# Attention and mixture-of-experts chain: V summed on VectorE, GpSimd and VectorE steps of the attention stage spread out, eight weight conversions moved

## The chip, the core and the metric

The kernel runs on one core of one Trainium2 chip. The metric is the device time of one launch in microseconds (us). The kernel before took 918.85 us, the median of three runs (917.21 to 921.72).

In what follows PE is TensorE, DVE is VectorE, ACT is ScalarE, POOL is GpSimd, and SP is SyncE, which here does nothing but issue DMAs. PEld is PE's weight load, which overlaps its matmuls.

## The reference, cut to what matters

Three stages, each fed by the one before it. Attention keeps only the keys whose six hash bits equal the query's; the first expert layer is a dense layer with a hard swish; the second layer picks two of eight experts per token.

```python
q_bucket = sum(((q @ proj) > 0) * 2**bits)          # 2 x 8 heads, 768 rows, 64 wide
scores = where(q_bucket == k_bucket, scale * q @ k.T, -1e9)
attn = exp(scores - scores.max(-1)); attn /= attn.sum(-1) + 1e-9
x = (attn @ v).reshape(1536, 512)
h = x @ w_in                                        # 512 -> 2048; these weights come as float64
x = (h * clip(h + 3, 0, 6) / 6) @ w_out             # 2048 -> 512
noisy = x @ w_gate + log1p(exp(x @ w_noise)) * noise
top2, w2 = two largest of noisy, softmax over them
out[n] = sum over the two experts e: w2 * (relu(x[n] @ w1[e]) @ w2[e])   # 8 experts, 512 -> 1024 -> 512
```

## The kernel before, in words

The order of instructions on PE, ACT, POOL and DVE is the order in which the Python code calls them (a manual schedule); each engine works through its own list in order, so an instruction that waits holds up all that stands behind it on its engine. SP's DMAs are put in order by the framework, and SP too issues them one after the other.

**Attention.** The 16 heads are taken in 8 pairs (NP = 8). A pair p takes 12 steps j = 0 to 11, so there are G = 96 steps g = 12p + j. The queries come in two halves of 384 (QH = 2), and each half takes six steps, one per block of 128 keys. In one step the main loop does this:

- `scores` (L469): PE multiplies keys and queries of the *next* step (L476, L477), and ACT takes the exponential of each half (L478). The S banks are two (NS = 2), so PE can be no more than one exponential ahead in each.
- `maxes` (L429): PE makes scores for a half that comes two halves later (L439), and DVE takes their row maximum (`tensor_reduce`, L443). The `mx` banks are two, so PE cannot start the maxima of step j+2 before DVE has reduced those of step j.
- in every odd step `av` (L481): PE multiplies the exponentials of two steps with V (L490). At the end of a half `finish` (L499) lets DVE add the uniform part, take the reciprocal r, and POOL write the normalised rows into `x_all` (L510).
- when a half's maxima are complete, `stab` (L445) makes the stabilisers on POOL in four short steps (L453 to L456); `stab2` (L458) has PE transpose them and ACT send them by DMA into two rows of A (L467, "A<-mr"), where the scores matmul L477 reads them.

Once per pair there are further steps, by their j: `load_cast` (0, POOL's DMA of B), `load_v` (2, the DMA of V and a POOL memset of V's ones columns), `bits_all` (4, hash bits), `lows` (6 and 7, a POOL subtraction of 128x768 each), `v_sum` (6, POOL: V summed over its six key blocks by five additions; the sum feeds the matmul of `v_sum2`), `uniform` (POOL, L342).

**Conversions.** The first layer's weights come as float64. `conv` (L186) turns half a 128-row slab into float32: it loads 512 KB (L189, "c_raw"), some steps later two ACT instructions (L200, L201) and one of DVE (L202), then one of DVE (L205) and POOL's addition (L206, 128x512), then DVE's L208, which reads what POOL wrote, and a store to DRAM (L211). There are 32. The kernel before does NU = 24 in the attention stage, one begun every three steps (g % 3 == 1), each advanced by one `yield` per step in `conv_step` (L216), and the other 8 in the first expert layer. In the attention stage a conversion's raw data take their buffer from the same pool of three as the float32 weight slabs of the first layer (tag "wr"); the first three slabs are loaded in steps 84, 85 and 86, and each gives its buffer back when `w_hi` (ACT, L229) and `w_lo` (DVE, L235) have split it, slab 0 in steps 88 and 89, slab 1 in 90 and 91, slab 2 after the last step.

**First expert layer.** 48 units u: three chunks of 512 tokens by 16 slabs, in two rounds: slabs 0 to FSPLIT-1 for each chunk, then the rest for each chunk. In a unit PE does `gemm1` for unit u+1 and `gemm2` for unit u, while ACT and DVE split slab u+2 and SP loads slab u+3. From u = 8 on a zero fill of DRAM buffers runs on SP's queue beside it (`prefill`). When a chunk is complete its routing follows in pieces (`routing`, L846).

**Second expert layer.** 10 parts by 8 slabs; the change touches only where the third chunk's routing is cut (ROUTE).

Of the kernel before, what the change touches and what calls it, by code (L numbers as in the profile page):

```python
# [20 lines left out]
EARLY = (224, 224)  # L21
ROW = 516
PF = (8, 2)
NU = 24
NS = 2
CL = 3
SL = CAP // 4
ROUTE = [(4, 0, 0), (1, 1, 0), (0, 1, 0), (4, 0, 0)]
NQ = len(EARLY)
PARTS = ([(e, 0, n, 2, False) for e, n in enumerate(EARLY)] + [(e, 0, CAP, 4, True) for e in range(NQ, 8)]  # L30
         + [(e, n, CAP - n, 2, False) for e, n in enumerate(EARLY)])
FSPLIT = 6
XA = 5
QJ = (1, 5)
XG = (75, 78, 81, 84)
# [9 lines left out]
def chain_kernel(ctx, tc, kq, vP, proj, wm, we, wgn, noise, out, dbg=None):  # L45
# [140 lines left out]
    def conv(n, cv_p, fine):  # L186
        k, hf = divmod(n, 2)
        raw = (wraw_p if fine else cv_p).tile([128, 512, 2], I32, name="c_raw", tag="wr" if fine else "c_raw")
        nc.sync.dma_start(raw, wm[k].bitcast(I32)[:, hf * 1024:(hf + 1) * 1024].rearrange("p (n t) -> p n t", t=2))  # L189
        for _ in range(CL if fine else 1):  # L190
            yield
        H, L = raw[:, :, 1], raw[:, :, 0]
        if fine:
            lu = wsp_p.tile([128, 1024], F32, name="c_lu", tag="wh")
            ta = wsp_p.tile([128, 1024], F32, name="c_ta", tag="wl")
            r, u, t, a = lu[:, :512].bitcast(I32), lu[:, 512:], ta[:, :512].bitcast(I32), ta[:, 512:]
        else:
            u, a = (cv_p.tile([128, 512], F32, name=n) for n in ("c_u", "c_a"))
            r, t = (cv_p.tile([128, 512], I32, name=n) for n in ("c_r", "c_t"))
        nc.scalar.activation(r, L.bitcast(U32), ACTF.Copy, scale=2.0 ** -29)  # L200
        nc.scalar.activation(u, H.bitcast(F32), ACTF.Abs)  # L201
        nc.vector.tensor_scalar(t, H, 3, 0x3FFFFFF8, op0=ALU.logical_shift_left, op1=ALU.bitwise_and)  # L202
        if fine:
            yield
        nc.vector.scalar_tensor_tensor(t, H, -0x40000000, t, op0=ALU.bitwise_and, op1=ALU.bitwise_or)  # L205
        nc.gpsimd.tensor_tensor(t, t, r, op=ALU.add)  # L206
        yield
        nc.vector.scalar_tensor_tensor(a, u, 2.0 ** -15, t.bitcast(F32), op0=ALU.is_ge, op1=ALU.mult)  # L208
        for _ in range(2 if fine else 1):
            yield  # L210
        nc.sync.dma_start(w32[k][:, hf * 512:(hf + 1) * 512], a)  # L211
# [68 lines left out]
    with actx:  # L280
# [35 lines left out]
        def load_v(p):  # L316
            t = T[p]
            t["V"] = op_p.tile([128, KT, 2, VW], F32, name="V", bufs=2)
            nc.sync.dma_start(t["V"], vP[p].rearrange("r k (h c) -> r k h c", h=2))
            nc.gpsimd.memset(t["V"][:, :, :, 64:], 1.0)  # L320

        def v_sum(p):
            t = T[p]
            V = t["V"].rearrange("p k h c -> p k (h c)")
            vr = sm_p.tile([128, 2 * VW], F32, name="vr")
            nc.gpsimd.tensor_tensor(vr, V[:, 0], V[:, 1], op=ALU.add)
            for k in range(2, KT):
                nc.gpsimd.tensor_tensor(vr, vr, V[:, k], op=ALU.add)
            t["vr"] = vr

        def v_sum2(p):
# [149 lines left out]
        def av(g):  # L481
            p, qh, kt = g // (2 * KT), g // KT % 2, g % KT
            t = T[p]
            if kt == 0:
                t["av"] = ps.tile([128, 512], F32, name="o", tag="o", bufs=1)
            for h in range(2):
                for i in range(KT // 2):
                    c = (h * (KT // 2) + i) * VW
                    for r in (0, 64):
                        nc.tensor.matmul(t["av"][r:r + 64, c:c + VW],  # L490
                                         E[g % NE][:, h, i * 128 + r:i * 128 + r + 64], t["V"][:, kt, h],
                                         start=kt == 0 and h == 0 and i == 0, stop=kt == KT - 1,
                                         tile_position=(0, r), skip_group_check=True)
            if kt == 0:
                at(g + 1, uniform, 2 * p + qh)
            elif kt == KT - 1:
                finish(p, qh, t["av"])

        def finish(p, qh, o):  # L499
            t = T[p]  # L500
# [6 lines left out]
            b, pp = divmod(p, NPB)  # L507
            i = b * KT + qh * (KT // 2)
            x = x_all[:, i:i + KT // 2, pp * 128:(pp + 1) * 128].rearrange("p a (h c) -> p h a c", h=2)
            nc.gpsimd.tensor_tensor(x, ov[:, :, :, 0:64],  # L510
                                    r.unsqueeze(3).to_broadcast([128, 2, KT // 2, 64]), op=ALU.mult)

        done = [0]

# [93 lines left out]
        for g in range(G):  # L608
# [51 lines left out]
                    move_k(p + 1)  # L660
            if p >= 1 and p + 1 < NP and j == 2:
                load_v(p + 1)
            if p + 1 < NP and j == 6:
                v_sum(p + 1)
                at(g + 5, v_sum2, p + 1)
            if p + 3 < NP and j == 6:
                load_raw(p + 3)
            if dbg is None or "x" not in dbg:
                conv_step(1 if g % 3 == 1 and cvn[0] < NU else 0, None, True)
            if g == 14:  # L670
                moe_consts()
            elif g == 16:
# [172 lines left out]

    def routing(c):  # L846
        for d in range(4):
            yield rt_trans(c, d)
        yield rt_logits(c)
        yield rt_noisy(c)  # L850
        yield rt_top(c)
# [2 lines left out]
        yield rt_pos(c)  # L854
        for t in range(4):
            rt_scatter(c, t)
            yield

    def w_next(k):
        if k + 3 < NMU + NEU:  # L860
# [136 lines left out]
    for u in range(NMU):  # L997
# [14 lines left out]
            w_lo(u + 2)  # L1012
        first(u + 1, lambda: w_lo(u + 2) if u else None)
        w_next(u)
        conv_step(1 - u % 2, cvm_p, False)
        route(1)
        if u + 1 < NMU:
            m1_second(u)
# [162 lines left out]
```

## Time and profile before

| | |
|---|---|
| median of 3 runs | 918.85 us |
| the profiled execution | 919.49 us, its span 917.8 us |
| PE busy | 848.0 us (92%) |
| DVE, ACT, POOL busy | 513.6, 423.1, 244.9 us |
| DMA moved | 151.74 MB, mean 165 GB/s |
| mean granted TensorE clock | 0.956 of full speed |

The table is one execution: the busy time of an engine, and the span from its first to its last instruction. The execution's time holds 1.69 us more than its span. A mean over the span hides that the stages differ: the attention stage is about the first 285 us, the first expert layer lies from there to about 560 us, and the rest is the second expert layer. The rows below cut the attention stage at the end of each pair's last V matmul.

### The profile page before, as it was taken

What the parts mean: (1) busy time and instruction counts of PE and PEld (TensorE: products, weight loads), DVE (VectorE), ACT (ScalarE), POOL (GpSimd) and SP (SyncE); (2) the same over time, 40 slices, a digit from 0 to 9 for tenths busy, and PEclk for the clock granted to TensorE, in tenths of its full rate; (3) what the DMA queues carried; (4) which work ended last, traced back from release to release, by engine and by line L of the source; (5) the groups of instructions that cost most, each with busy time, mean ns of one, the idle gap of its engine ahead of it and who ended that gap; (6) DMA issues with size and microseconds to landing.
All of it is one profiled execution on the core that took longest, in us unless ns stands there. A gap on an engine that the chain in (4) does not pass through costs nothing. (4 is left out here: it accounts for less than half of the span.)

```text
span 917.8 us, 15981 instructions
## 1 busy us (share of the span) xinstructions
PE 848.0 (92%) x6313; PEld 734.3 (80%) x6313; DVE 513.6 (56%) x859; ACT 423.1 (46%) x712; POOL 244.9 (27%) x286
## 2 busy tenths in 40 slices
PE   5889977787899999999999999889999999999993
PEld 2677766676788888888888888769999999999982
DVE  8657856565634666544665566645545445545561
ACT  4356544354555566544444444434433443443551
POOL 9166555274432121100012031521020120202211
PEclk8889998798999999999999999999999999999997
DMA  7655864945603459872225245696465666546671
GB/s 246 164 152 182 262 185 135 260 132 173 190 27 116 160 190 311 281 242 93 92 84 192 70 162 177 209 239 164 140 151 158 144 151 157 136 140 140 177 207 20
DMA packets 52347, 151.74 MB, mean 165 GB/s; under 512 B 8741, under 2 KB 9661, under 8 KB 52265
## 3 DMA queue, kind: packets, MB, share of 16 engines
q1 hardware_dynamic: 44393, 131.02, 46.6%
q0 software_dynamic: 7648, 19.53, 9.4%
q8 instruction: 51, 0.84, 0.4%
q14 instruction: 31, 0.25, 0.1%
q10 hardware_dynamic: 224, 0.10, 0.0%
HBM read 105.89 MB, written 32.41 MB: 151 GB/s over the span
## 5 line engine op out<-in xcount | busy, mean ns | idle before, releaser
L235 DVE TENSOR_TENSOR wl<-wr,wh 128x1024 fp32r<-128x1024 f32 (+1 forms) x128 | 155.9, 1218 | 126.2 <-ACT wh L229 126.2
L229 ACT CAST wh<-wr 128x1024 fp32r<-128x1024 f32 x128 | 134.4, 1050 | 120.0 <-PE S L946 75.8
L478 ACT ACTIVATE E<-S 128x384 f32<-128x384 f32 x192 | 90.5, 490 | 107.6 <-PE S L477 102.4
L976 POOL DMA_INDIRECT out_dram<-ot,ti x28 | 43.8, 1563 | 233.8 <-ACT ot L975 185.4
L443 DVE TENSOR_REDUCE mc<-mx 128x1 f32<-128x768 f32 x96 | 90.6, 951 | 19.7 <-PE mx L439 19.5
L439 PE MATMUL mx<-B,A 128*128 128x384 f32 x192 | 70.9, 383 | 27.3 <-DVE mc L443 24.9
L490 PEld LDWEIGHTS o<-V,E 128*64 128x64 f32 x2304 | 80.0, 151 | 13.8 <-issue 12.2
L273 DVE SCALAR_TENSOR_TENSOR g<-t,mx 128x512 f32<-128x512 f32 x47 | 32.4, 689 | 102.9 <-ACT t L272 102.9
L490 PE MATMUL o<-V,E 128*64 128x66 f32 x2304 | 86.8, 238 | 0.0
L701 PE MATMUL S<-wh,gh 128*128 128x512 f32 (+1 forms) x208 | 82.5, 397 | 0.0
L703 PE MATMUL S<-wh,gl 128*128 128x512 f32 (+1 forms) x208 | 81.6, 392 | 0.0
L702 PE MATMUL S<-wl,gh 128*128 128x512 f32 (+1 forms) x208 | 81.5, 392 | 0.0
L476 PE MATMUL S<-QX,KS 128*128 128x384 f32 x192 | 77.6, 404 | 2.5 <-ACT E L478 2.4
L477 PE MATMUL S<-A,B 128*128 128x384 f32 x192 | 68.8, 358 | 7.3 <-DMA A<-mr 7.3
L944 PE MATMUL S<-hh,wh 128*128 128x416 f32 x192 | 70.6, 368 | 0.0
L945 PE MATMUL S<-hh,wl 128*128 128x416 f32 x192 | 67.5, 352 | 0.0
L946 PE MATMUL S<-hl,wh 128*128 128x416 f32 x192 | 67.4, 351 | 0.0
L439 PEld LDWEIGHTS mx<-B,A 128*128 128x128 f32 x192 | 39.1, 208 | 34.6 <-DVE mc L443 30.6
L925 ACT ACTIVATE hh<-mx 128x416 fp32r<-128x416 f32 (+2 forms) x72 | 33.0, 459 | 65.6 <-PE mx L257 65.6
L272 ACT ACTIVATE t<-mx,half 128x512 f32<-128x512 f32 x47 | 32.3, 688 | 66.2 <-PE mx L257 66.2
L257 PE MATMUL mx<-xh,wh 128*128 128x512 f32 (+1 forms) x252 | 62.2, 369 | 0.6 <-ACT wh L229 0.6
L257 PE MATMUL mx<-xh,wl 128*128 128x512 f32 (+1 forms) x252 | 60.5, 362 | 0.6 <-DVE wl L235 0.6
(246 smaller groups left out, 1640.4 us busy)
## 6 DMA issues: line engine op xcount, KB each, us to landing
wr<-in_we_dram SPq DMA_DIRECT2D x80, 512.0 KB
wr<-w SPq DMA_DIRECT2D x48, 512.0 KB
c_raw<-in_wm_dram SPq DMA_DIRECT2D x32, 512.0 KB
xg<-pt SPq DMA_DIRECT2D x8, 838.5 KB
raw<-in_kq_dram SPq DMA_DIRECT2D x8, 768.0 KB
w<-c_ta SPq DMA_DIRECT2D x24, 256.0 KB
B<-in_kq_dram POOLq DMA_DIRECT2D x7, 768.0 KB, 8.2
xr<-xg SPq DMA_DIRECT2D x5, 838.5 KB
```

Of the source, the lines that this page charges most:

```text
L229: nc.scalar.copy(hi, W[k][0])
L235: nc.vector.tensor_tensor(lo[:, :n], W[k][0][:, :n], W[k][1][:, :n].bitcast(F32), op=ALU.subtract)
L257: nc.tensor.matmul(h, a[:, d * 128:(d + 1) * 128], b[:, d], start=i == 0 and d == 0, stop=i == 2 and d == 3)
L439: nc.tensor.matmul(pm[:, hf, :QW], t["A"][:, qh, q0:q0 + 128], t["B"][:, h, hf * QW:(hf + 1) * QW], start=True, stop=True)
L443: nc.vector.tensor_reduce(t["mc"][:, c:c + 1], pm[:, :, :QW], axis=AX.XY, op=ALU.max)
L476: nc.tensor.matmul(s[:, :QW], t["KS"][:, h, ks], t["QX"][:, qh, qs], start=True, stop=False)
L478: nc.scalar.activation(E[g % NE][:, h], s[:, :QW], ACTF.Exp, scale=0.125)
L490: nc.tensor.matmul(t["av"][r:r + 64, c:c + VW], E[g % NE][:, h, i * 128 + r:i * 128 + r + 64], t["V"][:, kt, h], start=kt == 0 and h == 0 ...
L701: nc.tensor.matmul(o, gh[:, ts], wh, start=first, stop=False)
L702: nc.tensor.matmul(o, gh[:, ts], wl, start=False, stop=False)
L703: nc.tensor.matmul(o, gl[:, ts], wh, start=False, stop=last)
L944: nc.tensor.matmul(o, wh[:, ds], hh, start=ft == 0, stop=False)
```

## The change

- The eight float64 conversions numbered 16 to 23 leave the attention stage (NU 24 to 16); the 16 that stay are begun every six steps (g % 6 == 3), and the first layer does 16 instead of 8. So that no slab is read before it is converted, the first round of slabs becomes longer (FSPLIT 6 to 7).
- Inside a conversion DVE's last step comes three steps after POOL's addition, not one.
- V's memset moves out of `load_v` into `v_sum`, `v_sum` moves from step 6 to step 8, and the five POOL additions become one DVE `tensor_reduce` over a strided view. `v_sum2` stays in step 11.
- POOL's write of the normalised rows is put off by one step: `finish` returns it, and it is called in the next step.
- Routing's third and fourth transposes go together, its last scatter ends the generator, and ROUTE's first entry is 3 instead of 4.

```diff
-NU = 24
+NU = 16
-ROUTE = [(4, 0, 0), (1, 1, 0), (0, 1, 0), (4, 0, 0)]
+ROUTE = [(3, 0, 0), (1, 1, 0), (0, 1, 0), (4, 0, 0)]
-FSPLIT = 6
+FSPLIT = 7
...
         nc.gpsimd.tensor_tensor(t, t, r, op=ALU.add)
-        yield
+        for _ in range(3 if fine else 1):
+            yield
         nc.vector.scalar_tensor_tensor(a, u, 2.0 ** -15, t.bitcast(F32), op0=ALU.is_ge, op1=ALU.mult)
...
             nc.sync.dma_start(t["V"], vP[p].rearrange("r k (h c) -> r k h c", h=2))
+
+        def v_sum(p):
+            t = T[p]
             nc.gpsimd.memset(t["V"][:, :, :, 64:], 1.0)
-
-        def v_sum(p):
-            t = T[p]
-            V = t["V"].rearrange("p k h c -> p k (h c)")
             vr = sm_p.tile([128, 2 * VW], F32, name="vr")
-            nc.gpsimd.tensor_tensor(vr, V[:, 0], V[:, 1], op=ALU.add)
-            for k in range(2, KT):
-                nc.gpsimd.tensor_tensor(vr, vr, V[:, k], op=ALU.add)
+            nc.vector.tensor_reduce(vr, t["V"].rearrange("p k h c -> p (h c) k"), axis=AX.X, op=ALU.add)
             t["vr"] = vr
...
             elif kt == KT - 1:
-                finish(p, qh, t["av"])
+                at(g + 1, finish(p, qh, t["av"]))
...
-            nc.gpsimd.tensor_tensor(x, ov[:, :, :, 0:64],
-                                    r.unsqueeze(3).to_broadcast([128, 2, KT // 2, 64]), op=ALU.mult)
+            return lambda: nc.gpsimd.tensor_tensor(
+                x, ov[:, :, :, 0:64], r.unsqueeze(3).to_broadcast([128, 2, KT // 2, 64]), op=ALU.mult)
...
-            if p + 1 < NP and j == 6:
+            if p + 1 < NP and j == 8:
                 v_sum(p + 1)
-                at(g + 5, v_sum2, p + 1)
+                at(g + 3, v_sum2, p + 1)
...
-                conv_step(1 if g % 3 == 1 and cvn[0] < NU else 0, None, True)
+                conv_step(1 if g % 6 == 3 and cvn[0] < NU else 0, None, True)
...
         for d in range(4):
-            yield rt_trans(c, d)
+            rt_trans(c, d)
+            if d != 2:
+                yield
...
             rt_scatter(c, t)
-            yield
+            if t < 3:
+                yield
...
-        conv_step(1 - u % 2, cvm_p, False)
+        conv_step(1 if u % 4 < 3 else 0, cvm_p, False)
```

What that does to the lists of three engines is shown by the order in which their instructions stand, an instruction to a row, with output and inputs by the program's names.

On POOL in the middle of a pair (the second one), from the end of step 5 to step 8, before; `x_all` is the write of the normalised rows, `c_ta` the conversion's addition, `ng`, `nr` and `u` the stabilisers, `KS` the two subtractions of `lows`, `vr` the sum of V:

```order
L510 TENSOR_TENSOR x_all<-ov,r 128x2x3x64
L206 TENSOR_TENSOR c_ta<-c_ta,c_lu 128x512
L453 TENSOR_SCALAR ng<-mc 128x6
L454 CAST nr<-ng 128x6
L455 TENSOR_TENSOR nr<-ng,nr 128x6
L456 TENSOR_SCALAR u<-mc 128x6
L360 TENSOR_TENSOR KS<-raw,B 128x768
L326 TENSOR_TENSOR vr<-V 128x132
L328 TENSOR_TENSOR vr<-vr,V 128x132 x4
L360 TENSOR_TENSOR KS<-raw,B 128x768
L342 TENSOR_TENSOR uf<-u,vs 128x396
L206 TENSOR_TENSOR c_ta<-c_ta,c_lu 128x512
```

and now, where `V` is the memset of its ones columns:

```order
L451 TENSOR_SCALAR ng<-mc 128x6
L452 CAST nr<-ng 128x6
L453 TENSOR_TENSOR nr<-ng,nr 128x6
L454 TENSOR_SCALAR u<-mc 128x6
L358 TENSOR_TENSOR KS<-raw,B 128x768
L508 TENSOR_TENSOR x_all<-ov,r 128x2x3x64
L358 TENSOR_TENSOR KS<-raw,B 128x768
L206 TENSOR_TENSOR c_ta<-c_ta,c_lu 128x512
L340 TENSOR_TENSOR uf<-u,vs 128x396
L324 MEMSET V 128x12x2
```

The five additions are gone, the stabilisers stand ahead of the write of `x_all`, one of two additions of a conversion is left, and the memset stands last.

On DVE over the same steps (the second pair, from the first half's end), before; `mc` is the row maximum, `ov` and `r` are the end of a half, the three rows of `c_ta` belong to conversions:

```order
L502 TENSOR_TENSOR ov<-o,uf 128x396
L505 TENSOR_SCALAR r<-ov 128x6
L506 RECIPROCAL r<-r 128x6
L205 SCALAR_TENSOR_TENSOR c_ta<-c_raw,c_ta 128x512
L443 TENSOR_REDUCE mc<-mx 128x1
L208 SCALAR_TENSOR_TENSOR c_ta<-c_lu,c_ta 128x512
L443 TENSOR_REDUCE mc<-mx 128x1
L202 TENSOR_SCALAR c_ta<-c_raw 128x512
L443 TENSOR_REDUCE mc<-mx 128x1
L205 SCALAR_TENSOR_TENSOR c_ta<-c_raw,c_ta 128x512
L443 TENSOR_REDUCE mc<-mx 128x1
L208 SCALAR_TENSOR_TENSOR c_ta<-c_lu,c_ta 128x512
```

and now, with the sum of V on it:

```order
L500 TENSOR_TENSOR ov<-o,uf 128x396
L503 TENSOR_SCALAR r<-ov 128x6
L504 RECIPROCAL r<-r 128x6
L441 TENSOR_REDUCE mc<-mx 128x1
L202 TENSOR_SCALAR c_ta<-c_raw 128x512
L441 TENSOR_REDUCE mc<-mx 128x1
L205 SCALAR_TENSOR_TENSOR c_ta<-c_raw,c_ta 128x512
L441 TENSOR_REDUCE mc<-mx 128x1
L326 TENSOR_REDUCE vr<-V 128x132
L441 TENSOR_REDUCE mc<-mx 128x1 x2
L209 SCALAR_TENSOR_TENSOR c_ta<-c_lu,c_ta 128x512
```

Before, one row maximum stands between a conversion's second and third DVE step; now three and the sum of V do.

On ACT near the end of the attention stage (steps 86 to 92 or so), before; `E` are the exponentials, `wh` the splits of the first weight slabs:

```order
L478 ACTIVATE E_132<-S 128x384 x2
L478 ACTIVATE E_133<-S 128x384 x2
L229 CAST wh<-wr 128x1024
L478 ACTIVATE E_134<-S 128x384 x2
L478 ACTIVATE E_135<-S 128x384 x2
L229 CAST wh<-wr 128x1024
L478 ACTIVATE E_132<-S 128x384 x2
```

and now:

```order
L476 ACTIVATE E_132<-S 128x384 x2
L476 ACTIVATE E_133<-S 128x384 x2
L230 CAST wh<-wr 128x1024
L476 ACTIVATE E_134<-S 128x384 x2
L476 ACTIVATE E_135<-S 128x384 x2
L200 ACTIVATE c_lu<-c_raw 128x512
L201 ACTIVATE c_lu<-c_raw 128x512
L230 CAST wh<-wr 128x1024
L476 ACTIVATE E_132<-S 128x384 x2
```

Two instructions of the conversion begun in step 87 now stand between the exponentials of step 91 and those of step 92. A further conversion (step 93) ends after the last step.

## Rows read from the trace of the kernel before

**Rows 1.** Stretches: length, busy PE, PEld, DVE, ACT, POOL; clock, DMA share, GB/s.

```profile
61.99:88.26 26.27, 25.77 (x381) 21.28 (x380) 21.01 (x32) 17.19 (x37) 16.84 (x30) 1.00 0.78 234
88.26:230.17 141.91, 115.94 (x1521) 95.30 (x1521) 88.18 (x128) 67.35 (x145) 73.30 (x101) 0.88 0.63 186
230.17:260.63 30.46, 27.72 (x378) 23.82 (x377) 19.43 (x29) 15.21 (x35) 13.64 (x23) 0.94 0.56 161
260.63:284.57 23.94, 23.02 (x353) 18.77 (x352) 6.27 (x10) 12.49 (x28) 5.98 (x8) 1.00 0.14 46
284.57:550.00 265.43, 265.43 (x1256) 218.73 (x1256) 150.40 (x264) 132.43 (x186) 33.63 (x30) 1.00 0.50 168
340.00:400.00 60.00, 60.00 (x268) 49.63 (x267) 34.57 (x47) 33.76 (x46) 5.15 (x4) 1.00 0.88 297
```

**Rows 2.** Waits from 20 to 285 us: us in total, times, longest us.

```profile
DVE c_ta L208 <- POOL c_ta L206: 59.5, 24, 6.6
...
POOL V L320 <- DMA V<-in_vP_dram: 25.2, 5, 7.6
PE mx L439 <- DVE mc L443: 23.5, 12, 3.3
```

**Rows 3.** Timeline at 157 us: start, us, instruction, idle before it.

```profile
158.49 0.69 DVE L208 SCALAR_TENSOR_TENSOR c_ta<-c_lu,c_ta 128x512 f32<-128x512 f32 x1 [4.41 <-POOL c_ta L206]
...
160.11 0.44 PE L439 MATMUL mx<-B,A 128*128 128x384 f32 x1 [2.44 <-DVE mc L443]
```

**Rows 4.** Groups of instructions, 40 to 280 us: count, busy us, mean ns.

```profile
L443 DVE TENSOR_REDUCE mc<-mx 128x1 f32<-128x768 f32 x81 | 76.9, 950 | 12.8 <-PE mx L439 12.7
...
L206 POOL TENSOR_TENSOR c_ta<-c_ta,c_lu 128x512 int32<-128x512 int32 x24 | 30.5, 1271 | 1.8 <-DVE c_ta L205 1.7
...
L360 POOL TENSOR_TENSOR KS<-raw,B 128x768 fp32r<-128x768 f32 x12 | 22.0, 1832 | 0.0
L510 POOL TENSOR_TENSOR x_all<-ov,r 128x384 f32<-128x384 f32 x15 | 17.5, 1164 | 88.2 <-DVE r L506 66.6 <-PE mx L439 14.8 <-PE S L477 6.7
...
L342 POOL TENSOR_TENSOR uf<-u,vs 128x396 f32<-128x396 f32 x15 | 13.8, 918 | 0.1
```

**Rows 5.** Timeline of POOL in pair 1: stabilisers, first subtraction, V's last additions.

```profile
81.14 0.23 POOL L453 TENSOR_SCALAR ng<-mc 128x6 f32<-128x6 f32 x1
...
82.40 1.83 POOL L360 TENSOR_TENSOR KS<-raw,B 128x768 fp32r<-128x768 f32 x1
...
84.92 2.47 POOL L328 TENSOR_TENSOR vr<-vr,V 128x132 f32<-128x132 f32 x4
```

**Rows 6.** Timeline: the stabilisers' DMA and the matmul that waits, pairs 1 and 3.

```profile
69.76 0.65 ACTq L467 DMA_DIRECT2D A<-mr  x1
...
74.93 0.44 PE L477 MATMUL S<-A,B 128*128 128x384 f32 x1 [0.50 <-DMA A<-mr]
...
130.60 0.64 ACTq L467 DMA_DIRECT2D A<-mr  x1
...
137.90 0.69 PE L477 MATMUL S<-A,B 128*128 128x384 f32 x1 [2.45 <-DMA A<-mr]
```

**Rows 7.** Timeline: a conversion's load, its first ACT step, and pair 7's steps.

```profile
162.49 1.56 SPq L189 DMA_DIRECT2D c_raw<-in_wm_dram  x1
...
165.67 0.66 ACT L200 ACTIVATE c_lu<-c_raw 128x512 int32<-128x512 uint32 x1 [2.58 <-DMA c_raw<-in_wm_dram]
...
274.60 1.23 DVE L235 TENSOR_TENSOR wl<-wr,wh 128x1024 fp32r<-128x1024 f32 x1
...
277.89 0.88 ACT L478 ACTIVATE E<-S 128x384 f32<-128x384 f32 x2 [1.16 <-PE S L477]
```

**Rows 8.** Timeline of the start: first row maxima, V's memset; PE in pair 0.

```profile
10.91 5.46 DVE L443 TENSOR_REDUCE mc<-mx 128x1 f32<-128x768 f32 x6 [0.90 <-PE mx L439]
...
11.39 0.13 POOL L320 MEMSET V<- 128x24 f32 x1
...
50.40 0.38 PE L464 MATMUL z<-ident,nr 128*12 128x128 f32 x1 [3.46 <-POOL nr L455]
```

More of the change, by code (lines that the diff above doesn't have):

```diff
@@ L319, in load_v @@
             nc.sync.dma_start(t["V"], vP[p].rearrange("r k (h c) -> r k h c", h=2))
-            nc.gpsimd.memset(t["V"][:, :, :, 64:], 1.0)
         def v_sum(p):
             t = T[p]
-            V = t["V"].rearrange("p k h c -> p k (h c)")
+            nc.gpsimd.memset(t["V"][:, :, :, 64:], 1.0)
             vr = sm_p.tile([128, 2 * VW], F32, name="vr")
-            nc.gpsimd.tensor_tensor(vr, V[:, 0], V[:, 1], op=ALU.add)
-            for k in range(2, KT):
-                nc.gpsimd.tensor_tensor(vr, vr, V[:, k], op=ALU.add)
+            nc.vector.tensor_reduce(vr, t["V"].rearrange("p k h c -> p (h c) k"), axis=AX.X, op=ALU.add)
             t["vr"] = vr
```

## The prediction

> **What bounds the kernel now.** I read the busy time by stretch first, then the waits, then the timeline at the waits.
>
> The stretches show where time can be won [rows 1]. From 284.57 to 550 us PE is busy all the time at the full clock: nothing that DVE, ACT or POOL save there can count. The attention stage is different. Pair 1 takes 26.27 us with PE busy for 25.77 at granted clock 1.00. Pairs 2 to 5 do the same work in 141.91 / 4 = 35.48 us, with PE idle for 26 of the 141.91 us and the clock at 0.88. The reader is to see that the matmuls are the same and that 9.2 us a pair are waits, and slow matmuls after them.
>
> The waits name the cause [rows 2]: PE waits 23.5 us for row maxima on DVE; DVE waits 59.5 us, 24 times, for POOL's addition of a conversion; POOL waits 25.2 us in five goes for V's DMA, because the memset of V stands in its list at step 2. So it is a chain of lists in order: POOL late, so DVE stuck at L208, so the maxima behind it late, so the `mx` banks not free. The timeline shows one link: DVE idle for 4.41 us, and PE for 2.44 soon after [rows 3].
>
> **The change part by part.** All differences are taken against the profiled execution, 919.49 us, which is 0.64 above the median of 918.85.
>
> *Pairs 2 to 5.* L208 now comes three steps after the addition instead of one. A step is about 2.1 us (26.27 / 12), so POOL may be 6 us late at no cost, and the 4.41 us wait goes. The memset leaves step 2, so POOL no longer stands behind V's DMA there. Half the conversions go: 2 additions a pair, 2 x 1.27 us off POOL [rows 4], and their DVE steps and 512 KB loads. What is left is a pair without these waits, and pair 1 is the measured example of one, with all four conversions still in it. So I start from 26.27 us, which contains a 0.50 us wait for the stabilisers' DMA [rows 6].
>
> What is late next is the sum of V. It is on DVE in step 8, waits for the memset on POOL, and the row maxima of steps 9 to 11 are queued behind it. From the start of step 6 POOL has to do: stabilisers 1.26 us (81.14 to 82.40 [rows 5]), two subtractions of 1.83, the write of `x_all` 1.16, the addition 1.27 and the uniform part 0.92 [rows 4]. That is 8.3 us. DVE comes to the sum after step 8's maxima, some 6 us after step 6 began, so it waits about 2 us. PE needs the bank of step 9 again in step 11, some 4.7 steps of 2.1 us after step 6 began, at about 9.9 us; it is free at 8.3 + 0.98 (the sum) + 0.95 (the maximum) = 10.2, or later where DVE's other steps come between. PE waits 0.3 to 0.9: I take 0.6. Its ends are 0 and 2.6 us a pair. Add 0.3 for raw data landing late on ACT, of which there is one 2.58 us wait in the rows and none in pair 1 [rows 7]. So a pair becomes 26.27 + 0.9 = 27.2 us, and four of them save 4 x (35.48 - 27.2) = 33.1.
>
> *The price of the sum itself* is not in the trace: DVE sums 792 elements a partition, six at a time, 528 bytes apart. The nearest row is the row maximum, 0.95 us for 768 contiguous elements [rows 4], which scales to 0.98. The other end is what POOL needed, 2.47 us for four of five additions [rows 5]; below 0.95 I expect nothing, since no DVE row of that length is shorter. I take 0.98, as the same operation on the same engine.
>
> The Trainium skill speaks against that value: "SBUF — State Buffer", section "Door 1: The DMA port swizzle", says that accesses which cross to a new 16-byte line each time pay a penalty, and here each does. No row of this kernel reads a long fp32 operand at such a stride, so the trace neither agrees nor disagrees; were the sum twice as long by it, the wait in step 11 would be 1.0 us longer and six pairs 6 us.
>
> *Pair 6* loses 2.7 us to idle PE and 0.06 x 30.46 = 1.8 to the clock [rows 1]; without both it takes 25.9: 4.5 saved. *Pair 1* gets the 0.9 of the new waits: -0.9. *Pair 0:* PE waits 3.46 us for stabilisers that stand behind a write of `x_all` and an addition [rows 8]. Now they stand ahead. Their own chain of 1.3 us remains, so 2.2 is won, and of slow matmuls after it I take 1.4, by the 1.8 of pair 6; less 0.6 for the sum: +3.0.
>
> *The start.* The first sum of V stands in DVE's list ahead of the first row maxima, which ran from 10.91 us; the memset that it needs came at 11.39 [rows 8]. DVE begins 0.6 late and then sums for 0.98: 1.6 us, of which POOL's shorter list gives a little back. -1.3. Ends: 0 and -1.6, or -3.1 with the long sum.
>
> *Pair 7.* Here the change adds a wait. The conversion of step 87 needs a buffer of the "wr" pool, and the three are held by the first weight slabs. It gets slab 0's, after the split on DVE in step 89, which ended at 274.60 + 1.23 = 275.83 [rows 7]. A raw load's ACT step came 3.2 us after its issue began (162.49 to 165.67 [rows 7]), so the data are there at about 279.2, and ACT does two steps of 0.67 and the next slab's 1.05 before the exponentials of step 92, at 281.6 to 282.2. They began at 277.89. Behind them stand PE's next scores. PE loses about 4.2 us, and after it the clock: pair 6, with 2.7 us idle, has a mean of 0.94, so that the lower level, 1.2 GHz, cost it 1.8 us [rows 1]; I add 2.2. -6.4, ends -3 and -9.
>
> *First expert layer.* ACT, DVE and POOL get eight conversions, beside a PE that is busy throughout; their cover is PE. From 340 to 400 us the DMA engines are already 0.88 busy at 297 GB/s [rows 1], with PE not waiting. Eight more loads and stores (768 KB each, 6.3 MB) lengthen that stretch by 6.3 MB / 297 GB/s = 21 us of transfer, which stays hidden as long as a slab loaded three units ahead is in time. I take -0.3 for the last conversion, which stands in front of slab 2's split with POOL's 1.27 us in it, while PE has two units' matmuls to do; ends 0 and -8. FSPLIT and the routing edits move the same instructions: 0.
>
> *Sum:* 33.1 + 4.5 - 0.9 + 3.0 - 1.3 - 6.4 - 0.3 = 31.7. 919.49 - 31.7 = 887.8, and 0.64 off for the median: 887.
>
> **The rivals.**
>
> *The wait moves to V's sum.* The long sum and POOL's queue make PE wait over 2 us in step 11 of each pair, and the clock falls as it does now. Then pairs 1 to 5 take what pair 6 takes today with one such wait, 30.46 us: 5 x (30.46 - 27.2) = 16.3 more, 903. For it: the memset is last of 8.2 us of POOL's list. Against: the conversions that left are worth more POOL time than PE's slack needs.
>
> *The stabilisers' DMA goes on as in pair 3.* There it took 7.3 us from issue to the waiting matmul, and 5.2 in pair 1 [rows 6]. I count on the shorter one, since fewer loads run beside it. If the longer one has another cause, PE keeps up to 1.95 us in each of pairs 2 to 5: 4 x 1.95 = 7.8 more, 895. Against: pair 1 moved 234 GB/s, more than pairs 2 to 5 did [rows 1], so load on the mean does not explain it; it may be what was issued just ahead.
>
> By the Trainium skill, "DMA: Bandwidth & Descriptors", section "Queues, rings and completion order", every DMA engine takes the queues in turn, a packet at a time, so a small DMA on ACT's queue should hardly feel loads on SP's; by that rule fewer conversions do not shorten it. The two rows, 5.2 and 7.3 us for the same 6 KB, show that something does.
>
> *Better than forecast.* The pairs reach 25.7 us (pair 1 less its 0.50 us), and pair 7's load lands early: 5 x 1.5 + 3 = 10.5 less, 876.
>
> *Slower than before: V lands late.* The sum on DVE stands behind V's DMA, through the memset. That DMA kept POOL waiting for up to 7.6 us [rows 2]. DVE's whole list is now behind it, row maxima first, where before DVE had another list. If SP gets to V so late that it lands 7 us or more after step 8's maxima, each pair loses 5 us of PE and the slow matmuls after it, and pairs 1 to 5 stay near 35.5: 5 x 8.3 = 41 is not won, 929. It decides from a landing some 2 us after step 8. Against: six steps, 12.6 us, now lie between the load and the sum, and V was never more than 7.6 us late at its own step.
>
> **How the numbers follow.** The forecast (880 to 897) has 0.56, the wait at V's sum 0.17, the stabilisers' DMA 0.10, better 0.12, slower 0.05. The 80% range takes in the better case and the wait at V's sum, and a little of the ends of pair 7 and of the first expert layer: 873 to 907. Half a percent, 4.6 us, is about what a measurement of this kernel can tell from no change. Only the V case ends above 923.4; of the first two rivals' chance I give 0.03 to times around 919, where bad ends come together: faster 0.92, same 0.03, slower 0.05.
>
> **What the changed profile would show.** Right: pairs 1 to 5 at 26 to 28.5 us each at granted clock near 1.00, DVE's wait for the addition near zero, PE's longest wait in the attention stage in pair 7 behind a conversion's raw load, and the stretch that is now 284.57 to 550 still busy throughout. Wrong: PE waiting for row maxima once a pair for over 2 us, with DVE idle before the sum of V (the first rival) and V's DMA named as the releaser (the last); PE waiting 2 us for "A<-mr" (the second); or PE idle in the first expert layer with a slab's DMA as releaser.

## The result, and the profile after

The changed kernel takes 887.41 us, the median of four runs (886.26 to 891.55), against 918.8 us before: ratio 0.9663, 95% interval 0.9622 to 0.9704. The forecast was 887 (873 to 907). The profiled execution took 888.51 us, its span 886.4. The work is the same (6313 matmuls in the trace, 151.74 MB moved); PE is busy with it for 834.2 us instead of 848.0, at a mean granted clock of 0.977 instead of 0.956.

The stretches are bounded as in [rows 1]. The bound lies at the begin, not at the end, of the 48 V matmuls that close a pair (one row of 1.62 us in the timeline); before and after, the pairs are equally long by either bound. The rows are pair 0, pair 1, pairs 2 to 5, pair 6, pair 7, and the first expert layer; columns as there.

```profile
24.14:58.44 34.30, 30.91 (x345) 24.90 (x345) 23.80 (x38) 14.33 (x32) 9.92 (x17) 0.87 0.51 144
58.44:85.70 27.26, 25.57 (x381) 21.20 (x380) 21.32 (x30) 14.55 (x33) 13.05 (x25) 1.00 0.70 197
85.70:192.15 106.45, 101.98 (x1522) 84.62 (x1521) 82.05 (x109) 57.56 (x129) 47.74 (x72) 1.00 0.70 192
192.15:217.67 25.52, 25.52 (x378) 22.43 (x377) 19.20 (x28) 15.47 (x35) 7.56 (x15) 1.00 0.41 117
217.67:248.71 31.04, 25.58 (x352) 20.79 (x351) 11.44 (x18) 15.07 (x32) 8.54 (x10) 0.89 0.28 95
248.71:518.00 269.29, 266.76 (x1258) 218.74 (x1258) 165.51 (x291) 142.03 (x204) 43.64 (x39) 1.00 0.58 193
```

Pairs 2 to 5 take 106.45 / 4 = 26.61 us instead of 35.48, at granted clock 1.00 instead of 0.88. Pair 1 grew by 1.0 us, and pair 7 from 23.94 to 31.04, at a clock of 0.89. The last V matmuls begin 35.86 us earlier (284.57 to 248.71), the span is 31.4 shorter: the later stages give 4.5 back.

The waits from 20 to 290 us, which answer to [rows 2]:

```profile
POOL ng L451 <- DVE mc L441: 93.2, 15, 12.9
...
PE mx L437 <- DVE mc L441: 9.8, 8, 2.6
DVE vr L326 <- POOL V L324: 9.6, 7, 1.5
...
ACT c_lu L200 <- DMA c_raw<-in_wm_dram: 4.4, 1, 4.4
...
DVE c_ta L209 <- POOL c_ta L206: 1.5, 1, 1.5
```

POOL, which stood behind V's DMA and the additions, now waits for others: 93.2 us for row maxima. DVE's 59.5 us for POOL's additions (at L208, which is L209 here) are 1.5, PE's 23.5 us for row maxima 9.8. What is new is DVE's wait for V's memset, seven times, ahead of the sum.

The timeline of after, at the start, in pair 3, in pair 7 and behind it (start, us, instruction, idle before it), which answers to [rows 3, 7, 8]:

```profile
11.54 1.59 DVE L326 TENSOR_REDUCE vr<-V 128x132 f32<-128x792 f32 x1 [1.54 <-POOL V L324]
...
130.84 1.83 POOL L358 TENSOR_TENSOR KS<-raw,B 128x768 fp32r<-128x768 f32 x1
...
130.97 2.25 DVE L205 SCALAR_TENSOR_TENSOR c_ta<-c_raw,c_ta 128x512 int32<-128x512 int32 x1
...
133.35 1.28 POOL L206 TENSOR_TENSOR c_ta<-c_ta,c_lu 128x512 int32<-128x512 int32 x1 [0.69 <-ACT mr L464]
...
135.38 0.12 POOL L324 MEMSET V<- 128x24 f32 x1
...
135.54 1.58 DVE L326 TENSOR_REDUCE vr<-V 128x132 f32<-128x792 f32 x1 [1.45 <-POOL V L324]
...
138.04 0.44 PE L437 MATMUL mx<-B,A 128*128 128x384 f32 x1 [1.14 <-DVE mc L441]
...
236.50 0.69 ACT L200 ACTIVATE c_lu<-c_raw 128x512 int32<-128x512 uint32 x1 [4.42 <-DMA c_raw<-in_wm_dram]
...
239.11 0.69 PE L474 MATMUL S<-QX,KS 128*128 128x384 f32 x1 [4.82 <-ACT E L476]
...
256.36 1.04 ACT L230 CAST wh<-wr 128x1024 fp32r<-128x1024 f32 x1 [4.34 <-DVE c_ta L209]
...
525.43 0.79 PE L915 MATMUL mx<-ident,x_all 112*128 112x112 f32 x6 [1.43 <-DMA x_all<-xg]
```

In pair 3 the chain of step 8 reads from top to bottom: memset last on POOL, DVE 1.45 us idle, the sum 1.58, and PE idle for 1.14 before the maxima of step 11. POOL itself stood idle for 0.69 us ahead of the addition at 133.35: the addition reads what DVE's L205 writes, and L205, which took 2.25 us, ended at 133.22. (The profile names ACT's `mr` for this wait, which the addition does not read and which was done at 132.90; for the same wait in pair 1 it names L205.) The rows at 236.50 and 239.11 are the wait that the change adds: ACT stands in front of step 87's raw data, the exponentials behind it are late, PE waits 4.82 us.

### The profile page after: what moved, and what is told of

It is laid out like the page before. It is cut to its first block, busy times and chain, and to the rows that moved or that the text cites. A ratio compares the mean times of both kernels' runs of the same rounds, so it can differ in the third digit from the quotient of the medians.

```text
span 886.4 us, 15973 instructions
## 1 busy us (share of the span) xinstructions
PE 834.2 (94%) x6313; PEld 722.3 (81%) x6313; DVE 529.1 (60%) x867; ACT 421.2 (48%) x712; POOL 215.8 (24%) x246
## 2 busy tenths in 40 slices
DMA packets 52348, 151.74 MB, mean 171 GB/s; under 512 B 8742, under 2 KB 9662, under 8 KB 52266
## 5 line engine op out<-in xcount | busy, mean ns | idle before, releaser
L488 PEld LDWEIGHTS o<-V,E 128*64 128x64 f32 x2304 | 73.5, 141 | 12.3 <-issue 9.6
L437 PE MATMUL mx<-B,A 128*128 128x384 f32 x192 | 66.7, 361 | 15.5 <-DVE mc L441 13.4
L488 PE MATMUL o<-V,E 128*64 128x66 f32 x2304 | 80.2, 227 | 0.0
L475 PE MATMUL S<-A,B 128*128 128x384 f32 x192 | 66.3, 345 | 0.0
L258 PE MATMUL mx<-xl,wh 128*128 128x512 f32 (+1 forms) x252 | 60.7, 363 | 0.0
```

What stands on the lines that cost most here:

```text
L258: nc.tensor.matmul(h, a[:, d * 128:(d + 1) * 128], b[:, d], start=i == 0 and d == 0, stop=i == 2 and d == 3)
L488: nc.tensor.matmul(t["av"][r:r + 64, c:c + VW], E[g % NE][:, h, i * 128 + r:i * 128 + r + 64], t["V"][:, kt, h], start=kt == 0 and h == 0 ...
```

## The experiments

Times are medians beside runs of the kernel before on the same chip (918.29 to 919.2 us). "Pairs 2 to 5" is the mean of the four, from one profiled execution, bounded as above; pair 7 and the begin of the last V matmuls are from the same execution.

| kernel | us | against before | ratio, 95% interval | pairs 2 to 5 | pair 7 | last V matmuls begin |
|---|---|---|---|---|---|---|
| before | 918.8 | | | 35.48 | 23.94 | 284.57 |
| after | 887.41 | -31.4 | 0.9663 [0.9622, 0.9704] | 26.61 | 31.04 | 248.71 |
| conversions alone | 911.79 | -6.5 | 0.995 [0.9918, 0.9982] | 31.00 | 31.08 | 273.83 |
| late L208 alone | 918.59 | +0.3 | 1.0007 [0.9986, 1.0029] | 33.95 | 23.94 | 282.80 |
| V's part alone | 902.02 | -16.3 | 0.9815 [0.9795, 0.9835] | 31.16 | 23.96 | 266.75 |
| late write alone | 920.73 | +2.4 | 1.0031 [1.0016, 1.0047] | 35.63 | 23.95 | 283.61 |
| all but conversions | 905.31 | -13.9 | 0.9856 [0.9809, 0.9903] | 32.17 | 23.96 | 268.44 |
| all but late L208 | 890.46 | -28.3 | 0.9685 [0.9668, 0.9703] | 27.22 | 31.20 | 252.64 |
| all but V's part | 898.90 | -19.9 | 0.9789 [0.9765, 0.9812] | 28.86 | 30.49 | 259.12 |
| after, NU 14 | 881.70 | -37.5 | 0.9575 [0.9535, 0.9614] | 27.09 | 23.94 | 245.36 |
| after, memset in step 5 | 888.85 | -30.4 | 0.9637 [0.958, 0.9694] | 27.14 | 30.34 | 249.50 |
| that, stabilisers sent earlier | 892.00 | -26.8 | 0.9705 [0.9685, 0.9724] | 27.83 | 31.88 | 253.20 |
| last version | 877.03 | -41.4 | 0.9541 [0.9513, 0.9569] | 27.58 | 24.55 | 241.30 |

### Each part alone

The theory was the prediction's chain of lists in order, of which each part takes away one link; the rival, that only the amount of conversion work in the stage counts.

The conversions' part:

```diff
-NU = 24
+NU = 16
...
-FSPLIT = 6
+FSPLIT = 7
...
-                conv_step(1 if g % 3 == 1 and cvn[0] < NU else 0, None, True)
+                conv_step(1 if g % 6 == 3 and cvn[0] < NU else 0, None, True)
```

The routing edits and the first layer's rate of conversions belong to this part and are not shown here.

> The kernel before with the conversions' part alone: NU 16, one begun every six steps, sixteen in the first expert layer, FSPLIT 7 and the routing edits; L208 still one step after POOL's addition, V's memset and its five additions still on POOL. Theory (a chain of lists in order, each part of the change takes away one link): the memset still holds POOL at step 2 until V lands, and each of the two L208 a pair can still be caught behind a late addition, so pairs 2 to 5 take 28 to 31 us each, against 35.5 before and 26.6 after; pair 7 shows its new wait of some 5 us behind c_raw (31 us); in all 895 to 907 us. Rival (what counts is only how much conversion work and traffic there is in the attention stage): pairs 2 to 5 at 26.5 to 27.2 us, as after, and 885 to 890 us.

Measured 911.79, above both ranges. Pairs 2 to 5 take 31.0 us: the rival's 26.5 to 27.2 is out. Pair 7's 31.08 is there. The waits, from 20 to 285 us:

```profile
DVE c_ta L208 <- POOL c_ta L206: 24.3, 6, 4.7
...
PE mx L439 <- DVE mc L443: 20.6, 8, 3.5
```

Fewer conversions leave 6 such stops of DVE instead of 24, but in each of pairs 1 to 5 one stop still makes PE wait 2.8 to 3.5 us. And pair 1, in which no stop was longer than 1.10 us before and none made PE wait [rows 1], takes 33.73 here: that it was undisturbed there was not a property of its work alone.

The late L208:

```diff
         nc.gpsimd.tensor_tensor(t, t, r, op=ALU.add)
-        yield
+        for _ in range(3 if fine else 1):
+            yield
```

> The kernel before with L208 three steps after POOL's addition instead of one, and nothing else. Theory: DVE's 59.5 us of waits for the addition nearly go, and with them most of PE's wait for row maxima; POOL's list is as long as before, so the stabilisers stay late in places. Pairs 2 to 5 at 27.5 to 31 us, pair 7 at 24 us, in all 888 to 900 us. Rival (amount of conversion work): no gain, 915 to 920 us.

Measured 918.59, no change: the time is the rival's, and the chain theory, as a sum of links, falls here. DVE's waits for the addition are gone, and others stand in their place:

```profile
POOL V L321 <- DMA V<-in_vP_dram: 32.4, 4, 11.6
ACT c_lu L200 <- DMA c_raw<-in_wm_dram: 32.1, 7, 7.7
DVE c_ta L202 <- DMA c_raw<-in_wm_dram: 16.6, 4, 4.6
```

The timeline of this run, SP's list and who waits behind it:

```profile
127.03 0.63 SPq L212 DMA_DIRECT2D w<-c_ta  x1
...
127.71 0.42 SPq L189 DMA_DIRECT2D c_raw<-in_wm_dram  x1
...
129.48 1.55 SPq L212 DMA_DIRECT2D w<-c_ta  x1
...
131.13 1.78 SPq L189 DMA_DIRECT2D c_raw<-in_wm_dram  x1
...
133.01 0.39 SPq L320 DMA_DIRECT2D V<-in_vP_dram  x1
...
133.80 0.67 ACT L200 ACTIVATE c_lu<-c_raw 128x512 int32<-128x512 uint32 x1 [7.36 <-DMA c_raw<-in_wm_dram]
...
142.72 0.12 POOL L321 MEMSET V<- 128x24 f32 x1 [10.89 <-PE mx L384]
```

The late L208 makes a conversion nine steps long, three times the spacing of three, so its store falls into the step in which a new load is begun and stands ahead of it on SP. Stores, loads and V come in one burst, ACT waits 7.36 us for raw data, and V's memset runs 9.7 us after V's issue. That the order on SP is the cause is read from these rows; it was not tried by itself.

V's part (memset and a DVE reduction in step 8; only the calls are shown):

```diff
-            if p + 1 < NP and j == 6:
+            if p + 1 < NP and j == 8:
                 v_sum(p + 1)
-                at(g + 5, v_sum2, p + 1)
+                at(g + 3, v_sum2, p + 1)
```

> The kernel before with V's part alone: the memset moved from step 2 to step 8, the sum from POOL to one DVE reduction in step 8. Theory: POOL's 25 us of waits for V's DMA go and 3 us a pair of additions leave its list, so the additions of conversions come in time more often; but four conversions a pair with L208 one step after the addition are still there. Pairs 2 to 5 at 28 to 31 us, in all 890 to 903 us. Rival (amount of conversion work): 1 us at most a pair, 914 to 920 us; it could cost, since DVE has 1.6 us more a pair and its own wait for the memset.

Measured 902.02, in the theory's range. DVE still stops at L208, but never for long:

```profile
DVE c_ta L208 <- POOL c_ta L206: 19.2, 23, 1.1
...
PE mx L436 <- DVE mc L440: 14.2, 7, 2.8
```

So the stops of up to 6.6 us in [rows 2] were POOL standing behind V's DMA and V's additions; which of the two weighs more was not tried. This is the largest single part.

The late write (`finish` called through `at(g + 1, ...)`; only the call is shown):

```diff
-                finish(p, qh, t["av"])
+                at(g + 1, finish(p, qh, t["av"]))
```

> The kernel before with the write of the normalised rows put off by one step, and nothing else. Theory: it moves 1.16 us of POOL's list behind the stabilisers twice a pair; the wait for stabilisers of 3.46 us in pair 0 gets shorter by 1 to 2 us, while the stops at V's memset and at L208 stay: pairs 2 to 5 at 34 to 36 us, in all 912 to 919 us. Rival (amount of conversion work): the same. A gain over 8 us would speak against both, and for POOL's order at the end of a half.

Measured 920.73, 2.4 us slower and 1.7 above the range's end. Its profiled execution does not show the loss: it took 918.44 us, 1.05 less than the one of before, with the last V matmuls 0.96 us earlier and the stages behind them as long as before (633.1 us against 633.2). Pair 0 ends 2.9 us earlier there, and pairs 1 to 6 take 1.9 of it back. Where the median loses is open; by itself the late write wins nothing.

### The parts together

The four alone sum to -6.5 + 0.3 - 16.3 + 2.4 = -20.1; together they give -31.4. So the next runs leave out one part each. The late write was not left out by itself.

All but the conversions (NU, FSPLIT, routing and `g % 3 == 1` as before):

> The changed kernel with the conversions as before: 24 in the attention stage, one begun every three steps, FSPLIT 6; the late L208, V's sum on DVE in step 8 and the late write stay. First theory (each part takes away its own link, whatever the others do): pairs 2 to 5 at 27 to 28.5 us, no wait behind c_raw in pair 7, no loss in the first expert layer: 878 to 886 us, faster than the changed kernel. Second theory, formed on the run with the late L208 alone, which won nothing and in which ACT waited 32.1 us in 7 goes for raw data: with a conversion every three steps the late L208 puts the store, on SP's list, in the step in which the next load is begun, so raw data land late, and only the wider spacing makes room for it: pairs 2 to 5 at 30 to 33 us and 896 to 906 us, no better than V's part alone (902).

Measured 905.31, the second theory's. Raw data are late again (waits, 20 to 285 us):

```profile
ACT c_lu L200 <- DMA c_raw<-in_wm_dram: 17.2, 5, 5.7
DVE c_ta L202 <- DMA c_raw<-in_wm_dram: 11.9, 5, 4.6
```

It is no better than V's part alone (902.02): at a spacing of three steps the late L208 and the late write win nothing beside it. The number of conversions and their spacing were changed together in all these runs, so which of the two makes the room is open.

All but the late L208:

```diff
-        for _ in range(3 if fine else 1):
-            yield
+        yield
```

> The changed kernel with L208's old place, one step after POOL's addition; conversions, V's sum and the late write as changed. First theory (chains of lists: DVE stuck at L208 is the main one): part of the gain is lost, pairs 2 to 5 at 27.5 to 29.5 us, 891 to 900 us. Second theory (the late L208 won nothing by itself; with two conversions a pair and a short list on POOL the addition is done in time anyway): pairs 2 to 5 at 26.5 to 27 us, 886 to 890 us.

Measured 890.46, between the two and next to the second: 3.0 us more than after. The intervals of the two ratios overlap, so the times alone do not show a difference; the traces do, 0.6 us in each of pairs 2 to 5, most of it in the wait of step 11, here that of pair 2:

```profile
113.19 0.44 PE L436 MATMUL mx<-B,A 128*128 128x384 f32 x1 [1.64 <-DVE mc L440]
```

It is 1.15 there in after. So with wide spacing the late L208 wins some 3 us, with narrow spacing nothing or less.

All but V's part:

> The changed kernel with V's memset in step 2 and its sum as five additions on POOL, as before; conversions, late L208 and late write as changed. Theory: V's part is the largest single one (16.3 us alone), since it is POOL standing behind V's DMA that makes all else late; without it pairs 2 to 5 take 28.5 to 31 us, 895 to 907 us. Rival (with half the conversions POOL has time enough to wait for V): pairs at 26.5 to 27.5 us, 885 to 890 us.

Measured 898.90, the theory's. Not row maxima but the stabilisers' DMA is late here (waits, 20 to 285 us):

```profile
POOL V L321 <- DMA V<-in_vP_dram: 24.1, 4, 8.0
...
PE S L478 <- DMA A<-mr: 14.3, 5, 3.8
```

Even with half the conversions, V's memset in step 2 and V's five additions on POOL together cost 11.5 us.

### Pair 7, and the length of the sum

```diff
-NU = 16
+NU = 14
```

> The changed kernel with 14 conversions in the attention stage instead of 16, so that the loads of steps 87 and 93 are not there; 18 in the first expert layer. Theory: pair 7 goes from 31.04 us back to 24 to 24.3, the 1.44 us wait for the last conversion's buffer goes too, and the first expert layer's PE stays busy: 7.1 + 1.4 = 8.5 us less, 878 to 880.5 us. Rival (the first layer has no room for more conversions: two more loads make a weight slab late): the gain shrinks to 0 to 5 us, 882 to 888 us.

Measured 881.70: 5.7 won of 8.5. Pair 7 is back at 23.94 and the 1.44 us wait behind it is gone, as the theory had it, and PE is busy through the first expert layer. What is missing lies elsewhere, and in this execution most of it is TensorE's clock. The stretches of this run, from 20 us to the end of pair 0, and pair 2:

```profile
20.00:60.23 40.23, 33.66 (x349) 27.00 (x349) 27.89 (x42) 15.77 (x35) 14.13 (x19) 0.79 0.51 134
...
87.50:115.66 28.16, 27.03 (x381) 22.67 (x380) 20.48 (x28) 14.41 (x33) 11.95 (x18) 0.94 0.73 198
```

Pair 2 takes 1.54 us more than in after (26.62) at 0.94, behind a wait of 1.72 us in the step before; pair 0 ends 1.79 later. In pair 2 PE is busy for 1.56 us more than in after, with the same idle time. In the first stretch the clock is 0.79, against 0.83 from 20 us to the end of pair 0 in after; PE is busy there for 1.2 us more and idle for 0.6 more, as one wait of 1.93 us has become 2.81. The other waits are those of after; more of the matmuls ran at 1.2 GHz.

V summed over neighbours instead of blocks:

```diff
-t["V"].rearrange("p k h c -> p (h c) k")
+t["V"].rearrange("p k h c -> p (k h c)").rearrange("p (a b) -> p a b", b=KT)
```

> The changed kernel with V summed over groups of six neighbours in memory instead of over its six key blocks, which leaves the sum meaningless; same operation, same 792 elements in, 132 out, contiguous instead of 528 bytes apart. Theory (the stride is the price): the reduction takes 0.95 to 1.1 us instead of 1.60. Rival (what costs is the many short groups, 132 outputs instead of one): it stays at 1.5 to 1.7 us.

The groups of instructions, 40 to 250 us (count, busy us, mean ns, idle before), after and then this run:

```profile
L326 DVE TENSOR_REDUCE vr<-V 128x132 f32<-128x792 f32 x7 | 11.2, 1597 | 9.6 <-POOL V L324 9.6
```

```profile
L326 DVE TENSOR_REDUCE vr<-V 128x132 f32<-128x792 f32 x7 | 6.8, 978 | 9.6 <-POOL V L324 9.6
```

1.60 us with the stride, 0.98 without: the stride is the price, and the 0.98 of the prediction is what the same elements cost side by side. With the short sum PE's wait in step 11 of pairs 2 to 5 is 0.38 to 0.53 us, where it is 1.03 to 1.16 in after; in pair 3:

```profile
136.25 0.45 PE L437 MATMUL mx<-B,A 128*128 128x384 f32 x1 [0.38 <-DVE mc L441]
```

The kernel ran once, in 886.74 us, and its pairs 2 to 5 take 26.34 us on the mean, 0.27 less than in after; in one of them a wait of 0.73 us for the stabilisers' DMA has come.

### The wait of step 11, and what takes its place

V's memset in step 5:

```diff
...
+            if p + 1 < NP and j == 5:
+                v_ones(p + 1)
             if p + 1 < NP and j == 8:
                 v_sum(p + 1)
```

`v_ones` is the memset, taken out of `v_sum`.

> The changed kernel with V's memset in step 5 instead of directly ahead of the sum in step 8; the sum stays where it is. Theory: PE's wait of 1.03 to 1.2 us in step 11 of six pairs comes from DVE waiting 1.45 us for the memset at the end of POOL's list; it goes, and pairs 1 to 5 take 25.4 to 25.9 us each: 5 to 7 us less, 880 to 882.5 us. Rival (the length of the sum, 1.6 us, is what makes the maxima late, whenever it starts; or the memset in step 5 holds POOL until V lands): 0 to 2.5 us less, 885 to 888 us.

The median, 888.85, lies 0.85 above the rival's range, and the rival's first reason is wrong: the wait of step 11 is gone although the sum still takes 1.6 us, and pairs 4 and 5 take 25.18 and 25.50 us, as the theory had it or better. Its second reason is there, since POOL waits 11.0 us in three goes for V's DMA, but no wait of PE names POOL for it. Another wait has come. The waits and one place of the timeline:

```profile
PE S L477 <- DMA A<-mr: 7.5, 4, 2.5
```

```profile
119.58 0.62 ACTq L467 DMA_DIRECT2D A<-mr  x1
...
126.69 0.44 PE L477 MATMUL S<-A,B 128*128 128x384 f32 x1 [2.46 <-DMA A<-mr]
```

The stabilisers' 6 KB need 7.1 us here. In after they never made PE wait; at the same place the DMA had landed when the matmul that reads its rows ran, 4.5 us after the issue:

```profile
120.00 0.62 ACTq L465 DMA_DIRECT2D A<-mr  x1
...
124.51 0.34 PE L475 MATMUL S<-A,B 128*128 128x384 f32 x1
```

From 121 to 124 us the DMA engines move 347 GB/s here and 126 in after. So the 1.1 us in step 11 likely let the large loads get out of its way; that was not tried by itself. Behind the 2.46 us the clock falls, and pair 3 takes 31.06. One of the four runs took 881.07, the others 888.65 to 889.45.

The stabilisers sent one step earlier:

```diff
-                d = 2 if hbd > 2 else 0
+                d = 1 if hbd > 2 else 0
```

> The run with V's memset in step 5, where PE's wait for row maxima in step 11 was gone but four waits of 1.3 to 2.5 us for the stabilisers' DMA (A<-mr) had come, now with the stabilisers' transpose and DMA one step after their sum instead of two. They were ready on POOL 4.7 us before the transpose. Theory (the small DMA takes 5 to 7 us beside the large loads at a pair's begin, and only its issue time is at fault): issued 2.1 us earlier, the four waits go, pairs 1 to 5 at 25.2 to 25.6 us, 879 to 883 us. Rival (the DMA lands when the large loads let it, whenever it is issued): the waits stay above 1 us each and the time at 886 to 890 us.

Measured 892.00, and both are wrong: the waits for A<-mr are gone, the time is worse. The timeline, in the second halves of pairs 2 and 3:

```profile
102.98 0.25 ACT L466 CAST mr<-z 12x128 fp32r<-12x128 f32 x1 [0.77 <-PE z L464]
...
103.91 0.62 ACTq L467 DMA_DIRECT2D A<-mr  x1
...
104.57 0.87 ACT L478 ACTIVATE E<-S 128x384 f32<-128x384 f32 x2 [1.34 <-PE mx L439]
...
105.11 0.44 PE L476 MATMUL S<-QX,KS 128*128 128x384 f32 x1 [1.11 <-ACT E L478]
...
133.09 0.87 ACT L478 ACTIVATE E<-S 128x384 f32<-128x384 f32 x2 [2.81 <-DMA A<-mb]
...
133.64 0.69 PE L476 MATMUL S<-QX,KS 128*128 128x384 f32 x1 [2.60 <-ACT E L478]
```

ACT issues that DMA 0.68 us after `mr` is ready, and the exponentials stand behind it. SP was issuing the hash bits' four A<-mb into the same tile from 99.58 to 102.89. That the DMA waited for them is not named in this pair, but it is in the next: there ACT is idle for 2.81 us, ended by A<-mb, PE then waits 2.60 us, and pair 3 takes 31.35 us at a clock of 0.89.

The last version takes the memset to step 7, sends early only the first half's stabilisers, moves the first sum of V behind the first exponentials, and has NU 14 (shown in part):

```diff
-                d = 2 if hbd > 2 else 0
+                d = 0 if hbd <= 2 else 1 if j < 6 else 2
...
+            if p + 1 < NP and j == 7:
+                v_ones(p + 1)
```

> The changed kernel with what the runs so far point to: 14 conversions in the attention stage; V's memset in step 7, when V is always there, instead of step 8; the first half's stabilisers sent one step after their sum instead of two, the second half's still after two (in the run before, sent earlier, their DMA held ACT behind the DMAs of the hash bits into the same tile); the first sum of V behind the first exponentials. Theory: against the run with 14 conversions (881.7) PE's wait of some 1.1 us in step 11 of six pairs goes without a new one, 6.6 us, and 1 us at the start: 872 to 876 us, pairs 1 to 5 at 25.2 to 25.7 us. Rival (what is taken off one wait in the attention stage is given to the next, as in the two runs before): pairs at 26.5 us or more and 879 to 884 us.

Measured 877.03 (873.87 to 880.77), between the two; it is the fastest here, 4.7 us below NU 14 alone, though the intervals of the two ratios overlap. Pairs 1 to 5 take 26.35, 26.73, 26.88, 25.82 and 30.87. In pair 5 the small DMA is late once more:

```profile
166.16 0.62 ACTq L467 DMA_DIRECT2D A<-mr  x1
...
175.93 0.44 PE L477 MATMUL S<-A,B 128*128 128x384 f32 x1 [3.27 <-DMA A<-mr]
```

9.8 us from issue to matmul. What holds it stays open.

## Why the prediction was right, point by point

*Pairs 2 to 5, 33.1 us predicted, 35.5 measured.* 27.2 a pair against 26.61. The waits that it named are gone. Of the two additions to pair 1's 26.27, PE's wait in step 11 was 1.03 to 1.16 us, not 0.6, and no raw data landed late there. POOL's list from the stabilisers to the memset, 8.3 us in the prediction, took 8.28 in pair 3 (127.10 to 135.38), but 0.69 of that is the wait behind L205, which the prediction did not have: that the two agree is luck. The 0.50 us for the stabilisers' DMA, which I left in, is not there; waits for it came back, longer, when the wait of step 11 was taken away. The start from pair 1 proved good, but its reason, that pair 1 is the work without waits, does not hold by itself: with one part alone pair 1 took 27.5 to 33.7.

*Which link counts.* The prediction gave most words to L208. Alone that edit won nothing, and in the whole it is worth some 3 us, which the times alone do not show clear of noise. V's part is worth 16.3 alone and 11.5 in the whole, the conversions 6.5 and 17.9. The late L208 needs the conversions' part, but that part does not need it: beside V's part and the late write it takes the time to 890.46 without it, 11.6 us below V's part alone. What the late write is worth in the whole was not tried.

*The sum of V, 0.98 us.* Mis-sized: 1.60. DVE waited 1.45 us for the memset where I had about 2, so wait and sum together took 3.05 us where I had 2.98: two errors that nearly cancel, by luck. PE's wait in step 11 still came out longer; with a sum of 0.98 us it was 0.38 to 0.53, near my 0.6. The page "SBUF — State Buffer" of the Trainium skill ("Door 1: The DMA port swizzle") says that an access that crosses to a new 16-byte line pays a penalty. That had the right sign; where the prediction tried twice as long, the runs give 1.60 / 0.98 = 1.6 times.

*Pairs 6, 1, 0 and the start.* 4.5 predicted for pair 6, 30.46 - 25.52 = 4.9 measured; -0.9 for pair 1, 26.27 - 27.26 = -1.0 measured. Pair 0 and the start together: 3.0 - 1.3 = 1.7 predicted, 61.99 - 58.44 = 3.6 measured. The 3.46 us wait for stabilisers [rows 8] is gone from pair 0.

*Pair 7, -6.4.* -7.1, by the wait named, at the place named: PE 4.82 us, and the clock at 0.89. Taking the load away gave it back.

*First expert layer, -0.3.* Mis-sized, and so may be the 0 for FSPLIT and the routing edits. The last conversion held slab 2's split by 4.34 us and PE by 1.44, not 0.3. With 1.43 us more behind the gathered tokens (the row at 525.43) and small ones, PE's named waits after the last V matmul grew from 7.1 to 10.6 us, 3.5 of the 4.5 us given back. Why the gathered tokens are later was not tried. The range of 0 to -8 held it.

*The sum.* 31.7 predicted, 919.49 - 888.51 = 31.0 in the profiled executions, 31.4 in the medians: pairs 2 to 5, pair 0 and pair 6 gave 4.7 more than forecast, pair 7 and the later stages took 4.9 more. So the number is closer than its terms, by luck.

*The rivals.* None came in the changed kernel. But the stabilisers' DMA, to which I gave 0.10, is what came as soon as the step 11 wait was taken away, and again in the run without V's part.

## What to carry to other kernels

In a chain of in-order lists the stop with the most idle time (59.5 us at L208) need not be the one to remove: ask what made its releaser late, here POOL, behind a DMA for a memset and with five additions in its list. Test parts both alone and left out, since an edit can need another: the longer conversion won nothing while a new one began every three steps. For a longer pipeline, count in which step its last DMA falls, against the loads on the same queue. A small wait may hide a late transfer; before taking it away, see what lands just in time.

## What the runs showed of the hardware

- A small DMA can take long while large ones run: the stabilisers' 6 KB took 7.1 and 9.8 us from issue to the matmul that waited, where the DMA engines were 0.99 (118 to 127 us, memset in step 5) and 0.92 busy (160 to 176 us, last version), and at most 4.5 us at the place shown of after. That the loads hold it was not tried by itself. "DMA: Bandwidth & Descriptors", section "Queues, rings and completion order", of the Trainium skill says that each DMA engine takes its queues in turn, a packet at a time. From that the prediction inferred that a small DMA should hardly feel the loads; these times do not bear the inference out.
- DVE's L205, with two operands in SBUF, took 2.25 us where POOL's subtraction of 128x768 ran beside it (the rows at 130.84 and 130.97), against 0.65 to 0.68 before the change; in after its mean is 1.26 us. The changed order puts the two side by side. "GPSIMD Engine Reference", section "1. Specifications", of the Trainium skill says that POOL's way to SBUF is shared with DVE's instructions of two SBUF inputs; the trace agrees. It held up POOL in turn: in pairs 1 to 5 POOL's addition, which reads what L205 writes, starts 0.68 to 0.69 us late (the row at 133.35), and the memset and the sum of V stand behind it.
- Waits of 1.7 to 3.3 us, once a pair, were followed in some pairs by a stretch at the lower clock (0.94 over a pair after 1.72 us), in others not (after 1.70 us, pair 2 of after stayed at 1.00). So nearly the same wait was followed by a pair of 28.16 us in one kernel and of 26.62 in the other.
